# The first batch's attention in an order written out by hand, and its value tiles in three transfers

## The chip, the cores and the metric

One core of one Trainium2 chip runs the whole program. The metric is the device time of one execution in microseconds.

## The reference

Attention over four batches of eight heads, with 512 local and 32 global rows of 64 values per head, and then two MLPs. A local row attends to the 32 global keys and to the local keys at most 32 positions away; a global row attends to all 544 keys. All in float32:

```python
s_ll = np.where(np.abs(pos[:, None] - pos[None, :]) <= 32, scale * q_l @ k_l.T, -1e9)
out_l = softmax([scale * q_l @ k_g.T, s_ll]) @ [v_g, v_l]
out_g = softmax(scale * q_g @ [k_g, k_l].T) @ [v_g, v_l]
x = attention output, heads side by side          # 2176 tokens x 512
xn = x / sqrt(mean(x * x) + 1e-6) * rms_g
y = (silu(xn @ w_gate) * (xn @ w_val)) @ w_out     # 512 -> 1536 -> 512
out = leaky(y @ w_in) @ w_out2                     # 512 -> 2048 -> 512
```

## The kernel before, in words

The attention works on units: a unit is one pair of heads of one batch, so a batch has four units (`NP`) and eight half units, each of two tiles of 128 query rows (`half_unit`, L235). A half unit k runs these steps. `scores` (L243) multiplies keys and queries into two PSUM banks `sc` (L158, through `together`); then, for each of four tiles, DVE adds the mask and takes the minimum of the negated scores (L258, into `s_ring` and `mx`), and ACT takes the exponential with its row sum (L261). `norm` (L265) adds up the doubled columns and scales by the reciprocal sums (DVE, L268 to L276). `turned` (L279) transposes on PE into `pp` (L288, L290) and copies to SBUF as `pt` (L295). `values` (L302) multiplies with the value tiles into `po` (L158) and copies to `x_loc` (ACT, L319). `s_ring` has three buffers, PSUM eight banks in this phase.

The global queries go by pairs of units (`global_pair`, L324): scores `sa`, `sb`, their maxima on DVE (L347 to L349), two exponentials on ACT, a copy of 32 columns (L356), transposes (L371, L372), value products `pz`, and a transpose back.

`load` (L209) brings a unit in: two halves of keys and queries (`kq`, 352 KB each, three buffers), a value tile `va` shifted by 32 rows (three transfers, four buffers), a second one `vb` (three transfers, three buffers), and four transfers of 8 KB of global values into one of three zeroed tiles `vz` (L233). All transfers are issued on SP's queue, in order; a transfer whose buffer is not yet free holds those behind it.

The first batch's steps are listed in `ORDER` (L451): S, N, T, V for a half unit's four steps, G for a global pair's, L for loads, D for squares. A "+" puts the steps behind it into a list (`later`) that the next `flush` empties, and `flush` is called within the steps, between matmuls and what follows them. The scheduler that places the instructions may still move them on each engine by its own reckoning, within the dependencies and the edges that `pinned` and `together` add. During this phase four weight chunks of the first MLP are also made (`convert`, L670, calling `narrow`, L102): each 512 KB of float64 words becomes 256 KB of float32 (one ACT and two DVE instructions), which is stored; then the chunk two or so steps ahead is fetched (L654). The first batch's normalisation is begun too: squares on ACT (L486), rows times gain on ACT (L492), sums on DVE (L503), the square root (L527) and its reciprocal.

Then `mlp1` (L892) begins with the gate product of its first step (`pg`, L934), which reads the rows times gain `xg` and the converted weights `wf`. The attention of batches 1 to 3 runs between the products of `mlp1`, by the slots of `PLAN` (L454); the second MLP follows. The scores of the first batch's second global pair come with the end of the first batch, its other steps inside `mlp1` (`LAST_PAIR`).

## Time and profile before

| | us |
|---|---|
| median of three runs | 954.7 |
| lowest, highest | 954.43, 955.53 |
| the profiled execution's own time | 955.33 |
| its span, first to last instruction | 953.6 |
| PE busy in the span | 914.3 (96%) |
| DVE, ACT, POOL busy | 617.4, 464.7, 5.1 |
| mean granted clock of TensorE | 0.983 of full speed |

A line of the profile names an engine (PE matmul, PEld weight load, DVE, ACT, POOL, SP), the line of the kernel, the operation, and what it writes and reads. "Idle before <-releaser" is the time for which the engine stood still just ahead of an instruction, and what ended that. Instructions of one engine overlap a little, so the step from one start to the next is often shorter than the duration. The granted clock is a share of 2.4 GHz; 0.5 is 1.2 GHz. In a table of windows the columns are the window, its length, the busy time (and count) of PE, PEld, DVE, ACT and POOL, the granted clock, the share of the DMA engines' time and the rate in GB/s.

### The profile page before, as it was taken

The page shows a single profiled execution, that of the slowest core. Times are in us where ns is not written, and L with a number is a line of the kernel's source. Part 1 is how long each engine was busy: PE and PEld are TensorE (multiplying, and loading weights), DVE is VectorE, ACT ScalarE, POOL GpSimd, SP SyncE. Part 2 cuts the span into 40 slices and gives each one's busy share as a digit, 9 for nine tenths or more (in the row PEclk, how much of TensorE's full clock was granted, in tenths as well). Part 3 has the DMA queues.
Part 4 walks back from the last instruction along what each step waited for, and adds up shares of the span by engine and source line. Part 5 has one row for each costly group of instructions (what it writes and reads, how often), then busy time and mean ns, then how long its engine had stood idle before and what let it go on. Part 6 is the DMA issues. An engine that isn't in the chain of part 4 may idle for free.

```text
span 953.6 us, 14727 instructions
## 1 busy us (share of the span) xinstructions
PE 914.3 (96%) x5172; PEld 742.9 (78%) x5172; DVE 617.4 (65%) x1380; ACT 464.7 (49%) x988; POOL 5.1 (1%) x26
## 2 busy tenths in 40 slices
PE   6588989999999999999999999999999999999998
PEld 4445767777777777777799999888888888888886
DVE  5469887679767687765678776676656434445332
ACT  5566666456445556553643443445544324334331
POOL 2000000000000000000000000000000000000000
PEclk9798989999999999999999999999999999999999
DMA  5788796679787999897377766777522176641113
GB/s 174 232 283 287 249 310 233 211 248 351 268 312 262 380 320 410 315 408 270 116 241 257 250 184 225 239 258 272 214 89 89 44 265 219 235 164 56 44 48 108
DMA packets 93354, 217.78 MB, mean 228 GB/s; under 512 B 15840, under 2 KB 31200, under 8 KB 91232
## 3 DMA queue, kind: packets, MB, share of 16 engines
q1 hardware_dynamic: 93280, 216.84, 65.9%
q8 instruction: 41, 0.67, 0.3%
q14 instruction: 33, 0.27, 0.1%
HBM read 150.21 MB, written 66.58 MB: 227 GB/s over the span
## 4 chain that ended last, share of the span: by engine, by line
PE 81%; DMA 2%; DVE 2%; ACT 1%; issue 1%; SPq 0%; DVEq 0%; ACTq 0%
PE o L85 18%; PE pg L85 9%; PE yp L85 8%; PE pv L85 8%; PE px L85 4%; PE py L85 4%; PE pz L85 4%; PE yt L85 4%; PE sc L158 2%; PE pw L85 2%; PE tz L85 2%; PE ty L85 2%; PE tx L85 2%; PE po L158 2%; PE po L85 1%; PE pr L85 1%
## 5 line engine op out<-in xcount | busy, mean ns | idle before, releaser
L85 PE MATMUL o<-wr,d 128*128 128x512 f32 x768 | 174.4, 389 | 0.0
L85 PEld LDWEIGHTS o<-wr,d 128*128 128x128 f32 x768 | 144.2, 188 | 29.9
L85 PE MATMUL pg<-xh,w 128*128 128x512 f32 x272 | 91.2, 416 | 1.3 <-ACT xh L89 1.3
L85 PE MATMUL pv<-xh,w 128*128 128x512 f32 x272 | 87.1, 400 | 0.0
L85 PE MATMUL yp<-hsh,w 128*128 128x512 f32 x288 | 84.0, 398 | 0.7 <-ACT hsh L89 0.7
L261 ACT ACTIVATE s_ring<-s_ring,mx 128x224 f32<-128x224 f32 x128 | 60.4, 473 | 44.7 <-DVE mx L258 44.5
L92 DVE TENSOR_TENSOR d<-h,d 128x512 fp32r<-128x512 f32 x64 | 42.1, 687 | 33.9 <-ACT d L89 33.9
L85 PEld LDWEIGHTS yp<-hsh,w 128*128 128x128 f32 x288 | 53.1, 188 | 13.8 <-issue 1.6
L85 PEld LDWEIGHTS pg<-xh,w 128*128 128x128 f32 x272 | 49.5, 193 | 17.9 <-issue 5.0
L85 PEld LDWEIGHTS pv<-xh,w 128*128 128x128 f32 x272 | 49.9, 189 | 11.7 <-issue 1.3
L158 PE MATMUL sc<-kq 64*128 64x224 f32 x256 | 43.0, 419 | 14.6 <-DMA kq<-kqv 12.9
L89 ACT CAST d<-h 128x512 fp32r<-128x512 f32 x64 | 38.2, 618 | 37.0 <-PE o L85 37.0
L85 PE MATMUL pg<-xl,w 128*128 128x512 f32 x136 | 54.6, 402 | 0.5 <-DVE xl L92 0.5
L89 ACT CAST w<-wf 128x512 fp32r<-128x512 f32 x68 | 41.6, 615 | 26.3 <-PE pv L85 16.1
L258 DVE CUSTOM_DVE_ANT_0 s_ring<-sc,masks 128x224 f32<-128x224 f32 x128 | 42.7, 385 | 17.3 <-PE sc L158 17.3
L85 PE MATMUL pv<-xl,w 128*128 128x512 f32 x136 | 53.4, 392 | 0.0
L85 PE MATMUL yp<-hsl,w 128*128 128x512 f32 x144 | 48.7, 398 | 1.1 <-DVE hsl L92 1.1
L85 PE MATMUL pz<-ysb,wr 128*128 128x512 f32 x192 | 49.2, 391 | 0.0
L92 DVE TENSOR_TENSOR w<-wf,w 128x512 fp32r<-128x512 f32 x68 | 46.3, 686 | 2.3 <-ACT w L89 2.2
L158 PEld LDWEIGHTS sc<-kq 64*128 64x128 f32 x256 | 28.0, 210 | 22.7 <-DMA kq<-kqv 13.5
L92 DVE TENSOR_TENSOR wr<-wr 128x1024 fp32r<-128x1024 f32 x16 | 19.6, 1225 | 39.7 <-ACT wr L89 39.6
L1240 ACT ACTIVATE h<-h 128x1536 f32<-128x1536 f32 x16 | 23.8, 1488 | 42.9 <-DVE h L883 42.9
(225 smaller groups left out, 1772.2 us busy)
## 6 DMA issues: line engine op xcount, KB each, us to landing
w<-w_dram SPq DMA_DIRECT2D x72, 512.0 KB, 5.6
w<-w SPq DMA_DIRECT2D x36, 512.0 KB, 5.2
w_dram<-w SPq DMA_DIRECT2D x36, 512.0 KB, 4.2
w64b<-w SPq DMA_DIRECT2D x32, 512.0 KB, 7.6
w_dram<-wr SPq DMA_DIRECT2D x8, 1792.0 KB, 7.9
wr<-w_dram SPq DMA_DIRECT2D x8, 1792.0 KB, 7.3
kq<-kqv SPq DMA_DIRECT2D x32, 352.0 KB, 5.2
w_f<-wf SPq DMA_DIRECT2D x36, 256.0 KB, 4.8
```

Source lines behind the costliest of these rows:

```text
L85: nc.tensor.matmul(dst, lhs[a], rhs[b], start=first and i == 0, stop=last and i == 2, skip_group_check=onto)
L89: nc.scalar.copy(hi, src)
L92: nc.vector.tensor_tensor(out=lo, in0=src, in1=hi.bitcast(F32), op=ALU.subtract)
L158: x = nc.tensor.matmul(dst, lhs, rhs, start=start, stop=stop, skip_group_check=bool(onto))
L258: nc.vector.tensor_tensor_reduce(out=sp, in0=sc[j][:, i * KW:(i + 1) * KW], in1=mask_of(t), scale=-scale, scalar=3.0e38, op0=ALU.add, op1= ...
L261: x = nc.scalar.activation(out=sp, in_=sp, func=AF.Exp, bias=mx[:, c:c + 1], scale=-1.0, accum_out=sm[:, c:c + 1])
L1240: nc.scalar.activation(out=out, in_=x, func=AF.Prelu, alpha=0.01)
```

## The change

The first batch runs under a manual schedule: on PE, DVE, ACT, SP and POOL the instructions keep the order of the text, from the first loads to the end of `first_batch`. The text is the new list `FIRST`, one line for each half unit k: its normalisation (n), the score products two half units ahead (p), the value products of the one before (v), its transposes (t), the copy of the large transposes on ACT (c), the copy of the values before (x), minima and exponentials two ahead (e), the copy of the small transpose, now always on DVE (d); then global steps, loads, squares (q), their sums (s), rows times gain (g), the halves of a weight conversion (a: one ACT and one DVE instruction, o: the last DVE instruction and the store), the table load (r), the root (R). Three of the four conversions move to the end of the list; the loads of unit 3's keys and queries come right after the scores of the first global pair, before the middle of the list.

The two value tiles of a unit become one tile with four buffers, filled by three transfers rather than six. Row 0 to 31 of its first half is no longer the rotated local row, so the global pairs multiply a zeroed stretch there (a POOL memset in place of a DVE copy) and take the last 32 local rows from `ve`, which grows from 32 to 64 rows and from two transfers to four. The small transfers leave SP: the global values `vz` of units 0 and 1 are issued by ACT at the very start, all others by POOL, and so are the `ve`. The transposed global weights are copied back into the tile that they came from. Unit 5's keys and queries are loaded after the list.

```diff
+        narrow_or(dst, *narrow_parts(pool, raw, name, bufs))
+
+    def narrow_parts(pool, raw, name, bufs=2):
         c = pool.tile([P, DM], F32, tag="nar_c", bufs=bufs, name="nc_" + name)
         r = pool.tile([P, DM], U32, tag="nar_r", bufs=bufs, name="nr_" + name)
         nc.scalar.activation(out=c, in_=raw[:, :, 1].bitcast(F32), func=AF.Prelu, scale=2.0 ** -112,
                              alpha=-2.0 ** 32)
         nc.vector.tensor_scalar(out=r, in0=raw[:, :, 0], scalar1=2.0 ** -29, scalar2=7.0,
                                 op0=ALU.mult, op1=ALU.min)
+        return c, r
...
-    anchors = {}
+    anchors, manual = {}, []
 
     @contextmanager
     def pinned(names):
 
         with ExitStack() as st:
             for x in names.split("+"):
-                if x:
+                if x and not manual:
...
-        shape, tag = (([P, HC], "kq0"), ([P, HC], "kq1"), ([P, NT, P], "va"), ([P, NT, P], "vb"))[part]
-        x = units[u, part] = at.tile(shape, F32, tag=tag, bufs=4 if part == 2 else 3, name=f"{tag}_{u}")
         if part < 2:
+            x = units[u, part] = at.tile([P, HC], F32, tag=f"kq{part}", bufs=3, name=f"kq{part}_{u}")
             nc.sync.dma_start(out=x, in_=kqv[b, p][:, part * HC:(part + 1) * HC])
             return
+        x = at.tile([P, 2, NT, P], F32, tag="v", bufs=4, name=f"v_{u}")
+        units[u, 2], units[u, 3] = x[:, 0], x[:, 1]
         v = kqv[b, p][:, 2 * HC:].rearrange("p (t d) -> p t d", d=P)
-        if part == 2:
-            nc.sync.dma_start(out=x[W:P], in_=v[0:P - W])
-            nc.sync.dma_start(out=x[0:W, 1:NT], in_=v[P - W:P, 0:NT - 1])
-            nc.sync.dma_start(out=x[0:W, 0], in_=v[P - W:P, NT - 1])
-            return
-        nc.sync.dma_start(out=x[0:W], in_=v_b[b, p][SG + W:KB])
-        nc.sync.dma_start(out=x[W:2 * W], in_=v[P - W:P])
-        nc.sync.dma_start(out=x[2 * W:P], in_=v[W:P - W])
+        nc.sync.dma_start(out=x[2 * W:P], in_=v[W:P - W].unsqueeze(1).to_broadcast([2 * W, 2, NT, P]))
+        nc.sync.dma_start(out=x[0:W], in_=v_b[b, p][SG:KB].rearrange("(y r) t d -> r y t d", y=2))
+        nc.sync.dma_start(out=x[W:2 * W], in_=v.rearrange("(y r) t d -> r y t d", r=W)[:, 0:P // W:P // W - 1])
+        if u >= NP:
+            spaced(u, nc.gpsimd)
+
+    def spaced(u, queue):
+        b, p = divmod(u, NP)
         units[u, "g"] = vz_ring[u % 3]
         for j in range(2):
             for i in range(2):
                 r, c = SG * (2 * j + i), slice(j * D, (j + 1) * D)
-                nc.sync.dma_start(out=vz_ring[u % 3][r:r + SG, i, c], in_=v_b[b, p][0:SG, 0, c])
+                queue.dma_start(out=vz_ring[u % 3][r:r + SG, i, c], in_=v_b[b, p][0:SG, 0, c])
...
-        def scores():
+        def products():
             kq = units[u, k % 2]
-            sc = [bank(f"sc{j}" + tg, 2 * NP <= k < 2 * NP + 2) for j in range(2)]
+            sc = hold["sc"] = [bank(f"sc{j}" + tg, 2 * NP <= k < 2 * NP + 2) for j in range(2)]
...
+        def scores():
+            products()
+            flush()
+            exps()
...
+            transposes(j)
+            flush()
+            copies(j)
...
+        def copies(j):
+            w = (4 if j == 0 else 1) * P
+            pp = hold["pp", j][:, 0:w]
+            pt = hold[j] = at.tile([P, w], F32, tag=f"pt{j}", bufs=2, name=f"pt{j}" + tg)
+            on_act = j == 0 or b == 1
+            x = (nc.scalar.copy if on_act else nc.vector.tensor_copy)(pt, pp)
+
+        def values():
+            gathered()
             flush()
-            pp = pp[:, 0:w]
-            pt = hold[j] = at.tile([P, w], F32, tag=f"pt{j}", bufs=2, name=f"pt{j}" + tg)
-            on_act = j == 0 or b == 1 or b == 0 and k % 2
-            x = (nc.scalar.copy if on_act else nc.vector.tensor_copy)(pt, pp)
-            if k == 2 * NP - 1 and j == 1:
-
-                with tc.issue_after(x.ins):
-                    nc.scalar.activation(out=early_root, in_=eps, func=AF.Sqrt)
-
-        def values():
-            po = bank("po" + tg)
+            kept()
...
+        parts = {"P": products, "E": exps, "N": norm, "T": lambda: [transposes(j) for j in range(2)],
+                 "C": lambda: copies(0), "D": lambda: copies(1), "V": gathered, "X": kept}
+        return scores, norm, turned, values, parts
...
-            hold["ve"] = [at.tile([SG, P], F32, tag=f"ve{n}", bufs=1, name=f"ve{n}" + tg) for n in range(2)]
+            hold["ve"] = [at.tile([G2, P], F32, tag=f"ve{n}", bufs=1, name=f"ve{n}" + tg) for n in range(2)]
             for n in range(2):
-                nc.sync.dma_start(out=hold["ve"][n], in_=v_b[b, p0 + n][0:SG, 0])
+                nc.gpsimd.dma_start(out=hold["ve"][n][0:SG],
+                                    in_=kqv[b, p0 + n][P - W:P, 2 * HC + (NT - 1) * P:])
+                nc.gpsimd.dma_start(out=hold["ve"][n][SG:G2], in_=v_b[b, p0 + n][0:SG, 0])
...
-            g = hold["g"] = at.tile([P, NK], F32, tag="sg", name="sg" + tg)
+            g = hold["g"] = at.tile([P, (NT + 1) * P], F32, tag="sg", name="sg" + tg)
...
-            nc.vector.tensor_copy(g[:, 0:SG], g[:, S:S + SG])
+            nc.gpsimd.memset(g[:, 0:SG], 0.0)
...
-            nc.tensor.transpose(ph[0:SG, 0:P], g[:, S + SG:NK], ident)
+            nc.tensor.transpose(ph[0:G2, 0:P], g[:, S:NK], ident)
             flush()
-            gt = hold["gt"] = at.tile([P, (NT + 1) * P], F32, tag="gt", bufs=1, name="gt" + tg)
+            gt = g
             nc.scalar.copy(gt[:, 0:S], pg[:, 0:S])
-            nc.scalar.copy(gt[0:SG, S:], ph[0:SG, 0:P])
+            nc.scalar.copy(gt[0:G2, S:], ph[0:G2, 0:P])
...
-            return [item(t) for t in ORDER.split()]
+            return lambda t: half[int(t[1])][4][t[0].upper()]() if t[0].islower() else one(t)()
...
-    ORDER = ("S0 S1+N0+Q0 T0+N1 S2 V0 T1+N2 S3 V1+D0+L33 G01+G0n+L30+L31 T2+N3 S4 V2 T3+N4 S5 V3+D1 G02 "
-             "T4+N5 S6 G03 V4 T5+N6 S7 V5+D2+L40+L41 G04 T6+N7 V6+L42+L43 T7+L50+L51 V7+D3+L52+L53")
+    def first_batch():
+
+        do = attention(0)
+        squares, root, _, _, gained = norms[0]
+        parts = {}
+
+        def weights(t):
+            g, k = int(t[1]), int(t[2])
+            if t[0] == "a":
+                parts[g, k] = narrow_parts(mb, wraw[g, k], f"{k}_{g}")
+                return
+            wf[g, k] = mp.tile([P, DM], F32, tag="wf", bufs=7, name=f"wf{k}_{g}")
+            narrow_or(wf[g, k], *parts[g, k])
+            kept_weights(g, k)
+
+        adds = {}
+
+        def squared(t):
+            c = int(t[1])
+            squares(c)
+            adds[c] = deferred.pop()
+
+        def spread_later(t):
+            root()
+            adds["root"] = deferred.pop()
+
+        more = {"q": squared, "s": lambda t: adds[int(t[1])](), "g": lambda t: gained(int(t[1])), "a": weights,
+                "o": weights, "r": lambda t: nc.scalar.activation(out=early_root, in_=eps, func=AF.Sqrt),
+                "R": spread_later, "z": lambda t: spaced(NP - 1, nc.gpsimd)}
+        for t in FIRST.split():
+            (more.get(t[0]) or do)(t)
+            flush()
+        return adds["root"]
+
+    FIRST = ("p0 e0 p1 e1 "
+             "n0 p2 t0 c0 e2 d0 Q0 "
+             "n1 p3 v0 t1 c1 x0 e3 d1 G01 L30 L31 "
+             "n2 p4 v1 t2 c2 x1 z0 e4 d2 q0 s0 g0 L40 L41 "
+             "n3 p5 v2 t3 c3 x2 e5 d3 G0n G02 "
+             "n4 p6 v3 t4 c4 x3 e6 d4 a00 "
+             "n5 p7 v4 t5 c5 x4 e7 d5 o00 G03 r0 L42 "
+             "n6 v5 t6 c6 x5 q1 g1 d6 G04 "
+             "n7 s1 v6 t7 c7 x6 q2 d7 L52 "
+             "v7 s2 x7 q3 s3 g2 R0 g3 a01 o01 a10 a11 o10 o11")
...
-            1: "2:T0+N1;5:V0+L22+L23+L20 S2", 2: "2:T1+N2;5:V1+L21 S3",
-            3: "2:T2+N3;5:V2+L32+L33+L30 S4", 4: "0:G01+G0n;2:T3+N4;5:V3+L31 S5",
-            5: "0:G02;2:T4+N5;4:G03;5:V4+L42+L43+L40 S6", 6: "0:G04;2:T5+N6;5:V5+L41 S7",
-            7: "2:T6+N7;5:V6+L52+L53", 8: "0:G11+G1n;2:T7;5:V7+L50+L51", 9: "0:G12;1:G13;3:G14"}
+            1: "2:T0+N1;5:V0+L22+L20 S2", 2: "2:T1+N2;5:V1+L21 S3",
+            3: "2:T2+N3;5:V2+L32+L30 S4", 4: "0:G01+G0n;2:T3+N4;5:V3+L31 S5",
+            5: "0:G02;2:T4+N5;4:G03;5:V4+L42+L40 S6", 6: "0:G04;2:T5+N6;5:V5+L41 S7",
+            7: "2:T6+N7;5:V6+L52", 8: "0:G11+G1n;2:T7;5:V7+L50+L51", 9: "0:G12;1:G13;3:G14"}
...
+        def gained(c):
+            if c == 0:
+                xg.append(mp.tile([P, KC, NX], F32, tag="xh", bufs=2, name="xg"))
+            x = nc.scalar.activation(out=xg[0][:, c, 0:n], in_=x_loc[0][:, c, 0:n], func=AF.Copy,
+                                     scale=gcol[:, c:c + 1])
+            anchors["xg"] = x.ins
...
-    for x in vz_ring:
-        nc.gpsimd.memset(x, 0.0)
-    load(0, 0)
-    load(0, 1)
-    load(0, 2)
-    load(0, 3)
-    with nc.allow_non_contiguous_dma(reason="512 gains, one column a chunk"):
-        nc.sync.dma_start(out=gcol, in_=rms_g.rearrange("(c p) -> p c", p=P))
-    constants()
-    global_queries(0)
-    for u in (1, 2):
-        for part in range(4):
+    engines = {mybir.EngineType.PE, mybir.EngineType.DVE, mybir.EngineType.Activation, mybir.EngineType.SP}
+    norms[0] = normalise(0, 0, BLOCKS1[0])
+    manual.append(True)
+    with tc.manual_schedule(engines=engines | {mybir.EngineType.Pool}):
+        for u in range(2):
+            nc.gpsimd.memset(vz_ring[u], 0.0)
+            spaced(u, nc.scalar)
+        for u, part in ((0, 0), (0, 1), (1, 0), (0, 2), (1, 1), (1, 2)):
             load(u, part)
-    load(3, 2)
-    for g in range(2):
-        for k in range(3):
-            if g < W64[k]:
-                fetch(g, k)
-    norms[0] = normalise(0, 0, BLOCKS1[0])
-    for n, item in enumerate(attention(0, norms[0][0])):
-        item()
-        if n < 2:
-            flush()
-        if n == 20:
-            convert(0, 0)
-        if n == 25:
-            convert(0, 1)
+        constants()
+        global_queries(0)
+        nc.gpsimd.memset(vz_ring[2], 0.0)
+        spaced(2, nc.gpsimd)
+        with nc.allow_non_contiguous_dma(reason="512 gains, one column a chunk"):
+            nc.sync.dma_start(out=gcol, in_=rms_g.rearrange("(c p) -> p c", p=P))
+        for part in range(3):
+            load(2, part)
+        load(3, 2)
+        for g in range(2):
+            for k in range(3):
+                if g < W64[k]:
+                    fetch(g, k)
+        spread = first_batch()
+    manual.clear()
     flush()
     early = attention(1)
-    convert(1, 0)
-    norms[0][1]()
-    spread = deferred.pop()
     last_pair[NP // 2 - 1][0]()
     later(last_pair[NP // 2 - 1][1])
-    convert(1, 1)
+    load(NP + 1, 0)
+    load(NP + 1, 1)
```

## Rows read from the trace of the kernel before

**Rows 1.** Windows by stage: PE, PEld, DVE, ACT, POOL busy us (count); clock, DMA.

```profile
4.00:28.80 24.80, 18.66 (x186) 13.77 (x186) 16.28 (x82) 17.69 (x66) 1.83 (x10) 0.93 0.67 205
28.80:37.50 8.70, 0.03 (x2) 0.03 (x2) 2.61 (x8) 1.92 (x5) 0.00 (x0) 0.62 0.74 243
37.50:56.80 19.30, 15.03 (x177) 10.85 (x177) 10.33 (x37) 13.13 (x37) 0.00 (x0) 0.82 0.69 194
56.80:140.00 83.20, 75.11 (x378) 51.07 (x374) 71.72 (x176) 55.62 (x131) 0.00 (x0) 0.92 0.86 285
140.00:953.00 813.00, 805.42 (x4436) 667.19 (x4436) 516.25 (x1077) 375.05 (x753) 0.00 (x0) 1.00 0.64 224
```

**Rows 2.** Timeline of PE: start us, us, what, count, idle before it and its releaser.

```profile
15.47 1.03 PE L158 MATMUL sc<-kq 64*128 64x224 f32 x8
...
22.11 0.34 PE L158 MATMUL po<-pt,va 128*64 128x64 f32 x4 [1.11 <-ACT pt L295]
...
23.24 0.66 PE L288 MATMUL pp<-ident,s_ring 128*128 128x128 f32 x4
...
23.93 1.03 PE L158 MATMUL sc<-kq 64*128 64x224 f32 x8
...
37.47 1.87 PE L158 MATMUL sc<-kq 64*128 64x224 f32 x8 [8.71 <-DMA kq<-kqv]
...
56.77 3.70 PE L934 MATMUL pg<-xg,wf 128*128 128x512 f32 x8
```

**Rows 3.** Timeline of SP's DMA issues: start us, us, line, what is loaded, count.

```profile
4.66 2.11 SPq L233 DMA_DIRECT2D vz<-v_b  x4
...
34.31 1.84 SPq L218 DMA_DIRECT2D kq<-kqv  x4
```

**Rows 4.** Waits of SP's queue, 0 to 110 us: total us, times, longest us.

```profile
SPq L233 <- DMA w<-w: 2.7, 2, 1.5
```

**Rows 5.** Timeline of DVE: start us, us, line, operation.

```profile
28.80 0.29 DVE L295 COPY pt<-pp 128x128 f32<-128x128 f32 x1 [0.86 <-PE pp L290]
29.01 0.16 DVE L268 TENSOR_SCALAR sm<-sm 128x4 f32<-128x4 f32 x1
...
30.43 0.42 DVE L115 TENSOR_SCALAR nr<-w 128x512 uint32<-128x512 uint32 x1
...
39.37 0.39 DVE L258 CUSTOM_DVE_ANT_0 s_ring<-sc,masks 128x224 f32<-128x224 f32 x1 [7.92 <-PE sc L158]
...
40.31 0.39 DVE L258 CUSTOM_DVE_ANT_0 s_ring<-sc,masks 128x224 f32<-128x224 f32 x1
```

**Rows 6.** Timeline of ACT: start us, us, line, operation.

```profile
6.48 0.48 ACT L261 ACTIVATE s_ring<-s_ring,mx 128x224 f32<-128x224 f32 x1 [4.46 <-DVE mx L258]
...
39.80 0.48 ACT L261 ACTIVATE s_ring<-s_ring,mx 128x224 f32<-128x224 f32 x1 [9.08 <-DVE mx L258]
...
41.68 0.35 ACT L391 ACTIVATE xg_g<-pz_g,gm_g 128x128 f32<-128x128 f32 x1
...
51.24 1.28 ACT L299 ACT_TABLE_LOAD   x1
...
55.73 0.63 ACT L486 ACTIVATE sq<-xl 128x512 f32<-128x512 f32 x1
```

**Rows 7.** Waits of DVE, 0 to 56.8 us: total us, times, longest us.

```profile
DVE gm_g L347 <- PE sa_g L158: 1.6, 1, 1.6
```

**Rows 8.** Windows of 2 us in which loads were queued: columns as in Rows 1.

```profile
12.00:14.00 2.00, 2.00 (x16) 1.39 (x18) 1.63 (x7) 0.31 (x1) 0.00 (x0) 0.55 1.02 295
18.00:20.00 2.00, 2.00 (x27) 1.38 (x23) 1.08 (x9) 1.92 (x9) 0.00 (x0) 1.00 1.05 344
26.00:28.00 2.00, 1.90 (x30) 1.46 (x30) 1.94 (x10) 1.97 (x9) 0.00 (x0) 1.00 1.00 408
```

**Rows 9.** Windows after PE's first pause and in the first MLP: columns as in Rows 1.

```profile
10.40:14.00 3.60, 3.41 (x21) 2.41 (x23) 2.57 (x12) 1.53 (x6) 0.00 (x0) 0.53 0.97 312
...
70.00:100.00 30.00, 27.01 (x130) 18.41 (x129) 29.54 (x80) 22.30 (x58) 0.00 (x0) 0.89 0.82 284
```

More of the change, by code (lines that the diff above doesn't have):

```diff
@@ L155, in together @@
             with ExitStack() as st:
-                if last is not None:
+                if last is not None and not manual:
                     st.enter_context(tc.issue_after(last))
@@ L249, in scores, with exps @@
                           kq[halves[j], i * KW:(i + 1) * KW], True, True) for i in range(2) for j in (1, 0))
-            flush()
+        def exps():
+            sc = hold["sc"]
             s = hold["s"] = s_ring[k % 3]
@@ L281, in turned, with transposes @@
                 flush()
+            transposes(j)
+            flush()
+            copies(j)
+        def transposes(j):
             s = hold["s"]
-            pp = bank(f"pp{j}" + tg)
+            pp = hold["pp", j] = bank(f"pp{j}" + tg)
             v = s.rearrange("p (c k) -> p c k", k=SC)
-            w = (4 if j == 0 else 1) * P
             if j == 0:
@@ L290, in turned, with gathered @@
                 nc.tensor.transpose(pp[:, 0:P], hold["sg"].rearrange("p c k -> p (c k)"), ident)
-            flush()
-            pp = pp[:, 0:w]
-            pt = hold[j] = at.tile([P, w], F32, tag=f"pt{j}", bufs=2, name=f"pt{j}" + tg)
-            on_act = j == 0 or b == 1 or b == 0 and k % 2
-            x = (nc.scalar.copy if on_act else nc.vector.tensor_copy)(pt, pp)
-            if k == 2 * NP - 1 and j == 1:
-                with tc.issue_after(x.ins):
-                    nc.scalar.activation(out=early_root, in_=eps, func=AF.Sqrt)
-        def values():
-            po = bank("po" + tg)
+        def copies(j):
[6 more added lines that the diff above has]
+            gathered()
+            flush()
+            kept()
+        def gathered():
+            po = hold["po"] = bank("po" + tg)
             halves = [slice(j * D, (j + 1) * D) for j in range(2)]
@@ L314, in values, with kept @@
             together(products)
-            flush()
+        def kept():
+            po = hold["po"]
             if b not in x_loc:
@@ L320, in values @@
             anchors[f"x{k}"] = x.ins
-        return scores, norm, turned, values
+        parts = {"P": products, "E": exps, "N": norm, "T": lambda: [transposes(j) for j in range(2)],
+                 "C": lambda: copies(0), "D": lambda: copies(1), "V": gathered, "X": kept}
+        return scores, norm, turned, values, parts
     def global_pair(w):
@@ L371, in turned @@
                 nc.tensor.transpose(pg[:, c * P:(c + 1) * P], g[:, c * P:(c + 1) * P], ident)
-            nc.tensor.transpose(ph[0:SG, 0:P], g[:, S + SG:NK], ident)
+            nc.tensor.transpose(ph[0:G2, 0:P], g[:, S:NK], ident)
             flush()
-            gt = hold["gt"] = at.tile([P, (NT + 1) * P], F32, tag="gt", bufs=1, name="gt" + tg)
+            gt = g
             nc.scalar.copy(gt[:, 0:S], pg[:, 0:S])
-            nc.scalar.copy(gt[0:SG, S:], ph[0:SG, 0:P])
+            nc.scalar.copy(gt[0:G2, S:], ph[0:G2, 0:P])
         def values():
-            gt = hold["gt"]
+            gt = hold["g"]
             pz = bank("pz" + tg)
@@ L383, in values @@
                 for n, r in enumerate(halves):
-                    rows = slice(0, P if c < NT else SG)
+                    rows = slice(0, P if c < NT else G2)
                     v = units[us[n], 2][:, c, :] if c < NT else hold["ve"][n]
@@ L488, in squares @@
                 hold["sum"] = mb.tile([P, NX], F32, tag="ssum", name=f"ssum{i}")
-            if i == 0:
-                if c == 0:
-                    xg.append(mp.tile([P, KC, NX], F32, tag="xh", bufs=2, name="xg"))
-                x = nc.scalar.activation(out=xg[0][:, c, 0:n], in_=x_loc[0][:, c, 0:n], func=AF.Copy,
-                                         scale=gcol[:, c:c + 1])
-                anchors["xg"] = x.ins
             def add():
@@ L549, in scaled @@
             later(lambda: low(xs[i][1][:, c, 0:n], xn[:, 0:n], xs[i][0][:, c, 0:n]))
-        return squares, root, scaled, hold
+        return squares, root, scaled, hold, gained
     NI = len(BLOCKS1)
@@ L677, in convert, with kept_weights @@
             narrow(mb, wf[g, k], wraw[g, k], f"{k}_{f}")
-        nc.sync.dma_start(out=w1_f32[f][k], in_=wf[g, k])
+        kept_weights(g, k)
+    def kept_weights(g, k):
+        nc.sync.dma_start(out=w1_f32[step_of(g)[1]][k], in_=wf[g, k])
         if step_of(g + W64[k])[0] == 0:
```

2 lines of the change are left out of this document (1 added, 1 removed).

## The prediction

> **What bounds the kernel now.** I read the windows by stage first, then PE's waits in the stage that is weakest, then the queue that feeds it. From 140 us on PE is busy 805.4 of 813 us [rows 1]: nothing in this change can gain much there. From 56.8 to 140 us, the first MLP's opening, PE is busy 75.1 of 83.2. Before 56.8 us it is busy 18.7 of 24.8, then 0.03 of 8.7, then 15.0 of 19.3 [rows 1], and nothing in its first 4 us. So about 23 of the first 56.8 us are PE's idle time, and all of that lies in the first batch's attention, which the change rewrites. The first MLP's first product `pg` starts at 56.77 us [rows 2]; I forecast by how much that start moves.
>
> Two things make the idle time. The large one is a single wait of 8.71 us for unit 3's keys and queries, which end it at 37.47 us [rows 2]. SP issued that load only at 34.31 us [rows 3]: it stood behind small loads, and SP was itself held by weight transfers that had not landed [rows 4]. The other is the pace. Between the score products at 15.47 and 23.93 us lie two half units, so one takes 4.23 us [rows 2], though PE's own work for one is 1.03 us of scores, 1.13 of value products (22.11 to 23.24) and 0.69 of transposes (23.24 to 23.93), 2.85 in all; PE stood 1.11 us ahead of the value products, for ACT's copy of the transposes just made [rows 2].
>
> **The change part by part.**
>
> *The order.* Each line of the new list gives the engines work of three half units, so that no engine waits for what was begun in the same line, the small copy `d` excepted. A line costs DVE 1.42 us of normalisation (29.01 to 30.43), four minima at 0.31 a step (39.37 to 40.31 is three steps), 1.25, and 0.21 for the small copy (28.80 to 29.01) [rows 5]: 2.88. PE needs 2.85, ACT 1.88 for the exponentials (39.80 to 41.68) [rows 6], which leaves it a microsecond for its two copies. So a line takes 2.9 us where it took 4.23, and DVE and PE share the limit. I walk along it:
> - Start. The first exponential came at 6.48 us [rows 6]. Now ACT first issues eight small transfers; at the 0.53 us that SP takes for one (four in 2.11) [rows 3] that is 4.2 us, with POOL's memset ahead of them and a table load of 1.28 [rows 6] about 6.5 us. No row shows a transfer issued by ACT: at best it costs nothing (the keys land no sooner), at worst I allow 1.5 us, the longest hold of SP's queue [rows 4]. I take 0, because SP's rows are the nearest.
> - Two half units of exponentials end at 6.5 + 2 x 1.88 = 10.3; the first normalisation starts after one, at 8.4. Lines 0 and 1 take DVE to 14.2.
> - The first global pair's scores hang on line 1. DVE waited 1.6 us for these products in the second pair [rows 7], and the maxima take 0.7: line 2 starts at 16.5, line 3 at 19.4, line 4, after 0.3 of global reciprocals, at 22.6.
> - Line 4 needs unit 3's keys. SP now issues them behind 7.3 MB (seven `kq` halves with this one, four value tiles, five weight chunks, small ones), all queued early. At the rates of windows in which such loads were queued, 295 GB/s for values, 344 for keys, 408 for weights [rows 8], 2.1 MB, 2.5 MB and 2.6 MB take 7.1, 7.3 and 6.4 us, the small ones about one; from 2 us on, and with one us to be reported, they land at 24.7. The wait of 8.7 us shrinks to 2.1.
> - Line 5 starts at 22.6 + 2.9 + 2.1 + 0.3 (half a conversion) = 27.9, line 6 at 31.4 (0.6 for the conversion's other half), line 7, without minima ahead, at 33.8.
> - The end has no neighbour to hide in: normalisation 1.4, a wait of 1.9 because ACT's table load (1.28) delays line 6's copies, transposes 0.7, copy 0.5, value products 1.1, copy 0.3, then two pairs of squares and gains at 1.04 each (55.73 to the `pg` that follows at 56.77 [rows 6, 2]): 41.8.
> - The second pair's scores, 2 us of PE, stood ahead of `pg` before; now they come when the root's products are out, at 40.3, so `pg` starts at 42.3.
> - Clock. In 10.4 to 14.0 us the granted clock was 0.53, the 1.2 GHz level, after a pause of PE; PE was busy 3.4 us there [rows 9], and at 2.4 GHz the same work takes about half. The pauses around 8 us and for unit 3's keys remain: I add 2 us. `pg` starts at 44.3.
>
> *Values in three transfers.* Bytes stay at 512 KB a unit. Three issues and four small ones leave SP for each unit, some 3.5 us at 0.5 each, and this is what lets the sum above take the loads as limited by bytes. Gain beyond that: none.
>
> *Small loads by POOL.* POOL issues four `vz` and four `ve` transfers and then the memset that the first pair's transposes wait for, at 21 us; its constants end at 7 us. At SP's 0.53 the eight take 4.2 us, done at 11.3. No row shows a transfer issued by POOL. They cost nothing as long as one takes under (21 - 7) / 8 = 1.75 us; `vz` of unit 3 is needed ten us later.
>
> *The rest.* The memset replaces a DVE copy of 0.2 us; `gt` in the place of `g` makes the next pair wait for value products that are long done; the wider `ve` product is the same instruction over 64 rows. All at nothing, within 0.5 us. Two conversions that came before `pg` now follow it: four DVE instructions, 1.9 us. `pg` itself (3.70 us [rows 2]) covers the one that the next product needs. DVE is full later (29.5 of 30 us between 70 and 100 us [rows 9]), so if they slip as far as that they cost 1.9. I take 0, for `pg` stands directly ahead.
>
> *Sum.* `pg` moves from 56.77 to 44.3 us, 12.5 us. The work behind it is the same, bound by PE and DVE, so I let it all move. The profiled execution took 955.33 us, so 942.8; it lies 0.6 above the median of 954.7, so 942.2 for the median, rounded to 942.5.
>
> **The rivals.**
>
> *A, loads set the pace.* If the early queue moves only 243 GB/s, the mean of the 8.7 us around the long wait [rows 1], 7.3 MB from 2 us on land at 32 us, 7.3 later than in the sum: 949.5. At 205 GB/s, the mean of 4 to 28.8 us [rows 1], they land at 37.6, as late as before, and nothing is gained. For it: these are the means there. Against it: in those stretches SP was issuing small loads or waiting, and windows with loads queued show 295 to 408 [rows 8]. Chance 0.15, of which 0.04 at no gain.
>
> *B, the gain is given back.* Weights reach the first MLP by the same DMA engines, busy 0.86 of that stage [rows 1], and DVE is full in 30 us of it [rows 9]. Should the shifted stage wait for weights or for the conversions, half is lost: 948.5. Against it: 285 GB/s [rows 1] is below what queued weights reach [rows 8]. Chance 0.10.
>
> *C, the order does not shorten the half unit.* If handovers between the engines keep a line at 4.2 us, only the long wait shrinks, by 6.6 us, less one us or so for the start: 949.5. For it: a fixed order stalls behind its slowest piece, and ACT issues transfers first. Against it: before, the wait was for a copy of the same half unit [rows 2], and that distance is doubled. Chance 0.07.
>
> *D, slower.* POOL's transfers run late in a row, with the memset behind them. If one takes c us, the first pair's transposes, and behind them all of PE's order, wait until 7 + 8c; the loss is 8c - 14, and over c = 3.3 it exceeds the 12.5 gained. At c = 4 the time is 960. Against it: the smallest issue in the rows is 0.53 [rows 3], and POOL has nothing else to do; for it, nothing in this trace, since POOL issues no transfer here. Chance 0.08.
> The Trainium skill, "SBUF — State Buffer", section "SBUF: two separate sides" (its trap "DVE blocks DMA"), says that a transfer from POOL's queue needs descriptors that POOL writes through a port which some DVE instructions lock, and gives 620 ns alone against about 3100 ns beside such an instruction. By that figure, taken for every one of the eight, the loss would be about 11 us and the time about 953; no run here shows it.
>
> **How the numbers follow.** A measurement of this kernel can tell about 0.2%, 1.9 us, from no change. The forecast has 0.60; its own range is 938 (no clock loss, no wait for unit 3) to 946 (ACT's start and the conversions at their upper bounds). With A, B and C the range is 937 to 951. Faster: 0.60 + 0.11 + 0.10 + 0.07 = 0.88. Within 0.2%: 0.04. Slower: 0.08.
>
> **What would show it.** Right: score products about 2.9 us apart, `pg` starting at 42 to 46 us, a wait for `kq` under 3 us, 56.8 to 140 us moved as a whole. Wrong: A by a wait for `kq` beyond 5 us; B by a stage from `pg` on that is longer than 83 us for the same work; C by score products 4 us apart without such a wait; D by PE or ACT waiting for POOL.

## The result, and the profile after

The changed kernel took 945.06 us (median of four runs, 942.53 to 946.54) beside 954.57 us for the kernel before on the same chip (954.1 to 955.53): a ratio of 0.9896, interval 0.9873 to 0.992. The profiled execution took 944.61 us, its span is 942.8, 10.8 shorter than before.

The windows by stage of the changed kernel, columns as in [rows 1]:

```profile
4.00:28.80 24.80, 17.97 (x157) 13.78 (x157) 17.25 (x82) 16.75 (x59) 8.22 (x24) 0.86 1.01 288
28.80:37.50 8.70, 7.34 (x70) 5.59 (x71) 3.65 (x17) 4.03 (x15) 2.21 (x4) 0.61 0.29 107
37.50:56.80 19.30, 14.83 (x156) 9.40 (x157) 13.82 (x41) 16.90 (x42) 5.95 (x13) 1.00 0.75 207
56.80:140.00 83.20, 77.94 (x445) 55.03 (x443) 76.99 (x196) 59.03 (x145) 7.77 (x17) 0.98 0.93 314
```

The hole of 28.8 to 37.5 us is nearly full, as forecast (PE busy 7.34 of 8.7 us, though at a clock of 0.61). But the stage from 56.8 us, which I had only meant to move, changed too: PE is busy 77.94 us of 83.2 (75.11 before), the clock is 0.98 (0.92), the DMA engines move 314 GB/s (285) [rows 1].

PE's timeline around the first batch's end, and the first product of the MLP's second block:

```profile
30.16 1.87 PE L156 MATMUL sc<-kq 64*128 64x224 f32 x8 [3.36 <-DMA kq<-kqv]
...
49.02 2.84 PE L1000 MATMUL pg<-xg,wf 128*128 128x512 f32 x6
...
53.41 1.16 PE L598 MATMUL rb<-rs,ident 128*128 128x128 f32 x8 [1.54 <-ACT sg_g L371]
...
55.27 3.60 PE L1000 MATMUL pv<-xg,wf 128*128 128x512 f32 x8
...
200.86 0.73 PE L85 MATMUL pg<-xh,w 128*128 128x512 f32 x2 [1.04 <-ACT xh L89]
```

`pv` and the second block's product in the kernel before:

```profile
61.20 3.60 PE L934 MATMUL pv<-xg,wf 128*128 128x512 f32 x8
...
210.13 0.73 PE L85 MATMUL pg<-xh,w 128*128 128x512 f32 x2 [1.04 <-ACT xh L89]
```

So `pg` moved by 7.75 us (from 56.77 [rows 2]), not by 12.5. It now runs in two parts, with the spread of the root (`rb`) and a wait of 1.54 us between, so that `pv` behind it moved by 5.93 only; the second block moved by 9.27. Of the 10.8 us, 5.9 come from the first batch, 3.3 from the stage behind it, 1.5 from what follows 200 us.

Where the first batch lost against the forecast: ACT's and SP's timelines at the start.

```profile
1.08 6.83 ACTq L232 DMA_DIRECT2D vz<-v_b  x8
...
2.47 0.44 ACTq L232 DMA_DIRECT2D vz<-v_b  x1
...
4.22 0.32 ACTq L232 DMA_DIRECT2D vz<-v_b  x1
...
7.94 1.28 ACT L262 ACT_TABLE_LOAD   x1 [7.94 <-DMA vz<-v_b]
9.23 0.48 ACT L262 ACTIVATE s_ring<-s_ring,mx 128x224 f32<-128x224 f32 x1
```

```profile
2.12 0.74 SPq L220 DMA_DIRECT2D v<-kqv  x1
3.94 0.34 SPq L221 DMA_DIRECT2D v<-v_b  x1
4.86 0.32 SPq L222 DMA_DIRECT2D v<-kqv  x1
6.70 0.35 SPq L215 DMA_DIRECT2D kq<-kqv  x1
7.90 0.62 SPq L220 DMA_DIRECT2D v<-kqv  x1
...
21.13 5.09 SPq L215 DMA_DIRECT2D kq<-kqv  x4
```

The first row holds all eight of ACT's transfers; the two below it are the fourth and the fifth of these. One issue took ACT 0.32 to 0.44 us, but it stood between the last ones, so the eight took 6.83 us. The table load could only follow: the first exponential came at 9.23 us instead of 6.48 [rows 6]. While ACT issued, SP's own issues stood up to 1.8 us apart. DVE's timeline shows the walk: the start of the normalisation in lines 0 and 2 to 7.

```profile
11.23 0.17 DVE L274 TENSOR_SCALAR sm<-sm 128x4 f32<-128x4 f32 x1 [2.53 <-ACT s_ring L262]
...
21.05 0.16 DVE L274 TENSOR_SCALAR sm<-sm 128x4 f32<-128x4 f32 x1
...
24.03 0.16 DVE L274 TENSOR_SCALAR sm<-sm 128x4 f32<-128x4 f32 x1
...
27.32 0.15 DVE L274 TENSOR_SCALAR sm<-sm 128x4 f32<-128x4 f32 x1
...
35.77 0.17 DVE L274 TENSOR_SCALAR sm<-sm 128x4 f32<-128x4 f32 x1
...
39.35 0.16 DVE L274 TENSOR_SCALAR sm<-sm 128x4 f32<-128x4 f32 x1
...
41.82 0.16 DVE L274 TENSOR_SCALAR sm<-sm 128x4 f32<-128x4 f32 x1
```

POOL had issued everything early, at 0.50 to 0.53 us each (the memset is what the first pair's transposes wait for):

```profile
10.19 0.50 POOL L357 DMA_DIRECT2D ve_g<-v_b  x1
10.67 0.14 POOL L375 MEMSET sg_g<- 128x32 f32 x1
```

### The profile page after: what moved, and what is told of

It is laid out like the page before. It is cut to its first block, busy times and chain, and to the rows that moved or that the text cites. A ratio compares the mean times of both kernels' runs of the same rounds, so it can differ in the third digit from the quotient of the medians.

```text
span 942.8 us, 14764 instructions
## 1 busy us (share of the span) xinstructions
PE 911.3 (97%) x5172; PEld 742.1 (79%) x5172; DVE 618.0 (66%) x1376; ACT 463.1 (49%) x984; POOL 50.4 (5%) x122
## 4 chain that ended last, share of the span: by engine, by line
PE 78%; DMA 4%; DVE 1%; ACT 1%; issue 1%; SPq 1%; ACTq 0%; DVEq 0%
PE o L85 18%; PE yp L85 8%; PE pg L85 8%; PE pv L85 7%; PE px L85 4%; PE py L85 4%; PE pz L85 4%; PE yt L85 4%; DMA w64b<-w 2%; PE pw L85 2%; PE tz L85 2%; PE ty L85 2%; PE tx L85 2%; PE sc L156 2%; PE po L156 2%; PE po L85 1%
## 5 line engine op out<-in xcount | busy, mean ns | idle before, releaser
L85 PE MATMUL yt<-hst,w 128*128 128x320 f32 x288 | 42.9, 310 | 1.0 <-DMA w<-w_dram 0.7
```

Of the source, the lines that this page charges most:

```text
L85: nc.tensor.matmul(dst, lhs[a], rhs[b], start=first and i == 0, stop=last and i == 2, skip_group_check=onto)
```

## The experiments

All ratios are to the kernel before, run on the same chip with the kernel named. "Changed" is the changed kernel, 0.9896.

### 1. The small values at the start by POOL

```diff
-            spaced(u, nc.scalar)
...
-        spaced(2, nc.gpsimd)
+        for u in range(3):
+            spaced(u, nc.gpsimd)
```

> The eight small transfers of units 0 and 1 are issued by POOL behind its constants, not by ACT. Theory (ACT's issues set the late start: they took 6.83 us, and SP was held with few loads in flight beside them): the first exponential comes at about 6.5 us instead of 9.23, SP's first loads are issued without holds, and everything behind moves by 2.5 to 4 us: 941 to 942.5 us. Rival (the start is bound by when keys and masks land, ACT only happened to be busy): the first exponential stays near 9 us and the time at 945. Second rival (POOL now issues 16 transfers in a row, and the first value products wait for the global values): the value products of unit 0 wait for POOL's transfers, gain under 1 us.

944.08 us, ratio 0.9886 [0.9859, 0.9914], which the intervals do not part from the changed kernel. The start is mended, and the gain is swallowed at the next wait. ACT's and PE's timelines:

```profile
6.33 0.48 ACT L262 ACTIVATE s_ring<-s_ring,mx 128x224 f32<-128x224 f32 x1 [4.31 <-DVE mx L259]
```

```profile
30.01 1.87 PE L156 MATMUL sc<-kq 64*128 64x224 f32 x8 [6.92 <-DMA kq<-kqv]
```

PE now waits 6.92 us for unit 3's keys instead of 3.36 and goes on at nearly the same time as before, 30.01 us (30.16). The start was late, but the keys set the pace: `pg` starts at 48.23 us, 0.8 earlier. The second rival's sign showed too: PE waited 1.45 us for the global values that POOL now issues.

### 2. The first five weight chunks behind unit 3's keys

```diff
-        for g in range(2):
-            for k in range(3):
-                if g < W64[k]:
-                    fetch(g, k)
...
-             "n1 p3 v0 t1 c1 x0 e3 d1 G01 L30 L31 "
+             "n1 p3 v0 t1 c1 x0 e3 d1 G01 L30 L31 f00 f01 f02 f10 f11 "
```

> The first five weight chunks are fetched behind unit 3's keys and queries instead of ahead of them. Theory (unit 3's keys land late because 2.6 MB of weights are queued ahead): PE's wait of 3.36 us for them falls under 1 us, and the 1.2 GHz stretch that follows it goes too (1.5 us more): 940 to 942 us. Rival (they are late because SP may issue them only once the first global pair's scores are done, so the order of the queue behind that changes nothing): the wait stays above 2.5 us, 944 to 946. Second rival: the weights, now late themselves, hold the conversions and the first MLP; slower than 946.

939.5 us, ratio 0.9836 [0.9803, 0.987], a little under the theory's 940 to 942. In PE's timeline the products of unit 3 follow at once:

```profile
26.56 1.03 PE L156 MATMUL sc<-kq 64*128 64x224 f32 x8
...
47.22 3.18 PE L1000 MATMUL pg<-xg,wf 128*128 128x512 f32 x6
```

They take 1.03 us, not 1.87: without the pause PE also keeps the 2.4 GHz level. The five chunks, 2.6 MB, were what stood between the keys and their place in the queue. But `pg` starts only 1.8 us earlier than in the changed kernel (47.22, 49.02): behind a later wait of 1.66 us, for ACT's copy of the transposes, PE ran the end of the batch at the 1.2 GHz level (granted clock 0.50 from 42 to 47 us).

### 3. All small loads back on SP

```diff
-            spaced(u, nc.gpsimd)
+            spaced(u, nc.sync)
...
-                nc.gpsimd.dma_start(out=hold["ve"][n][SG:G2], in_=v_b[b, p0 + n][0:SG, 0])
+                nc.sync.dma_start(out=hold["ve"][n][SG:G2], in_=v_b[b, p0 + n][0:SG, 0])
```

> All small transfers (global values and the global pairs' rows) go back to SP's queue; the order by hand and the three value transfers stay. Theory (SP's queue is short of issue time early, and small loads hold the large ones there; and the stage after 57 us gained because SP no longer carries them): the keys of units 2 and 3 land later, PE waits 3 to 6 us more, but ACT starts 2.7 us earlier; together 945 to 949 us, with the stage from the gate product to 140 us some 3 us longer than now. Rival (where the small transfers are issued does not matter beyond ACT's late start): 942 to 943.

954.55 us, ratio 0.9992 [0.9976, 1.0008]: the whole gain is gone, more than the theory's 945 to 949, with the written order and the three transfers still in place. `pg` still starts 3.7 us earlier than in the kernel before (53.06, 56.77), and nothing of that reaches the end. PE's waits of 0 to 140 us:

```profile
PE sc L156 <- DMA kq<-kqv: 14.4, 3, 7.6
```

### 4. Minimum steps one half unit ahead instead of two

```diff
-    FIRST = ("p0 e0 p1 e1 "
-             "n0 p2 t0 c0 e2 d0 Q0 "
-             "n1 p3 v0 t1 c1 x0 e3 d1 G01 L30 L31 "
...
+    FIRST = ("p0 e0 "
+             "n0 p1 t0 c0 e1 d0 Q0 "
+             "n1 p2 v0 t1 c1 x0 e2 d1 "
...
```

> Score products, minima and exponentials run one half unit ahead instead of two, all else as in the changed kernel. Theory (the distance of two is what takes the handovers between the engines out of the line): a line takes 4 us or more where it now takes 3.0 to 3.5, eight lines cost 5 to 8 us more: 949 to 953. Rival (the distance does not matter, only the fixed order and the loads do): within 1.5 us of 945.

950.36 us, ratio 0.9949 [0.9929, 0.9969]. PE's timeline shows lines 4.97 and 4.98 us apart, with PE waiting for DVE's normalisation:

```profile
18.80 0.63 PE L298 MATMUL pp<-ident,s_ring 128*128 128x128 f32 x4 [0.52 <-DVE s_ring L280]
...
23.77 0.63 PE L298 MATMUL pp<-ident,s_ring 128*128 128x128 f32 x4 [2.23 <-DVE s_ring L280]
...
34.26 0.63 PE L298 MATMUL pp<-ident,s_ring 128*128 128x128 f32 x4 [1.72 <-DVE s_ring L280]
...
39.24 0.63 PE L298 MATMUL pp<-ident,s_ring 128*128 128x128 f32 x4 [2.23 <-DVE s_ring L280]
```

In a written order the distance of two is worth 0.5%, with a reservation: this list also moves the first global pair's scores and unit 3's loads one line later, and what these cost was not separated. `pg` starts at 57.58 us, later than in the kernel before (56.77), and the time is shorter all the same.

### 5. Experiments 1 and 2 together

The edit is the two diffs above.

> Both at once: the first eight small transfers by POOL, and the first five weight chunks behind unit 3's keys. Theory (the early start was worth under a microsecond alone only because the wait for unit 3's keys swallowed it; without that wait it comes through): first exponential at 6.4 us, no wait for keys over 2 us, the gate product starts 2 to 3 us earlier than with the keys first alone (47.2 us), at 44 to 45.5; ratio to the kernel before 0.979 to 0.983. Rival (the tail, bound by ACT, sets the end, so the start is still hidden): the gate product stays at 47, ratio 0.983 to 0.986.

938.39 us, ratio 0.9816 [0.9773, 0.9859]; `pg` at 42.36 us, no wait for unit 3's keys. Taken alone, the start had moved `pg` by 0.8 us; with the keys in place nothing swallows it, and line 7 begins 1.7 us earlier than in experiment 2 (DVE's first instruction of it at 34.77 us, 36.49 there). `pg` is 4.9 us earlier, but most of what lies behind line 7 is the clock: the second pair's scores, in experiment 2 and here, ran at the 1.2 and at the 2.4 GHz level.

```profile
44.75 1.95 PE L156 MATMUL sa_g<-kq,bd 128*64 128x256 f32 x8
```

```profile
41.01 1.06 PE L156 MATMUL sa_g<-kq,bd 128*64 128x256 f32 x8
```

In device time the interval does not part this kernel from experiment 2.

### 6. The new loads alone, in the scheduler's order of before

The kernel before with three value transfers and the small loads issued by POOL; the order of the first batch is left as it was.

```diff
+        nc.sync.dma_start(out=x[2 * W:P], in_=v[W:P - W].unsqueeze(1).to_broadcast([2 * W, 2, NT, P]))
...
-                nc.sync.dma_start(out=vz_ring[u % 3][r:r + SG, i, c], in_=v_b[b, p][0:SG, 0, c])
+                queue.dma_start(out=vz_ring[u % 3][r:r + SG, i, c], in_=v_b[b, p][0:SG, 0, c])
...
+            spaced(u, nc.gpsimd)
```

> The loads of the change alone (three value transfers, small loads by POOL, the global pairs' changes), with the order of the kernel before left to the scheduler. Theory A (half or more of the gain is SP's queue set free): unit 3's keys are issued before 28 us, PE's longest wait falls from 8.7 to 3 to 5 us, and the first MLP runs as in the changed kernel: ratio 0.989 to 0.995. Theory B (the order by hand is what gains; loads only let it): ratio 0.997 to 1.0. Theory C (the order gives nothing once the loads are free): ratio 0.988 to 0.991, as the changed kernel.

947.17 us, ratio 0.9896 [0.986, 0.9931]: the same ratio as the changed kernel, without its order. And this with a bad start of its own: POOL put its transfers among the masks, the last of which was done at 13.3 us, and PE's timeline shows 7.52 us of waiting for it:

```profile
14.63 1.08 PE L292 MATMUL pp<-ident,s_ring 128*128 128x128 f32 x4 [7.52 <-DVE s_ring L278]
```

SP issued unit 3's keys at 22.74 us (34.31 before [rows 3]), and PE never waited for them.

### 7. Only the later small loads back on SP

```diff
-            spaced(u, nc.gpsimd)
+            spaced(u, nc.sync)
...
-                nc.gpsimd.dma_start(out=hold["ve"][n][SG:G2], in_=v_b[b, p0 + n][0:SG, 0])
+                (nc.sync if w else nc.gpsimd).dma_start(out=hold["ve"][n][SG:G2], in_=v_b[b, p0 + n][0:SG, 0])
```

> The first batch as in the changed kernel, but the small loads of all later units and global pairs on SP's queue again. Theory (the stage behind the gate product gained some 4 us because small loads that wait for a buffer no longer stand in SP's queue ahead of weights): the gate product starts at 49 us as now, and the stage up to 140 us takes 3 to 5 us longer: ratio 0.993 to 0.996. Rival (that stage gained by where the conversions stand, or by the clock): ratio 0.988 to 0.991, as the changed kernel.

953.96 us, ratio 0.9962 [0.9941, 0.9982]. About 6 us are lost (0.9962 against 0.9896). In the profiled runs 1.5 us of the loss lie ahead of `pg` (50.52 us, 49.02 in the changed kernel) and 4.1 between `pg` and the second block (206.46, 200.86). The longest wait of a small load in SP's queue, 0 to 140 us:

```profile
SPq L355 <- PE pz_g L156: 10.5, 1, 10.5
```

A load of 16 KB waits 10.5 us on SP until PE has read the buffer that it overwrites, and everything that SP was to issue stands behind it. Yet this wait is not the price. In the changed kernel SP stands as long in the same stretch, ahead of the first conversion's store, for DVE. That kernel's wait (26 to 40 us) and its issues, then the issues here:

```profile
SPq L744 <- DVE sm L274: 12.2, 1, 12.2
```

```profile
39.45 0.33 SPq L744 DMA_DIRECT2D w_f<-wf  x1
...
90.43 1.42 SPq L717 DMA_DIRECT2D w<-w  x2
```

```profile
39.79 0.34 SPq L355 DMA_DIRECT2D ve_g<-kqv  x1
...
40.85 0.35 SPq L744 DMA_DIRECT2D w_f<-wf  x1
...
96.59 1.26 SPq L717 DMA_DIRECT2D w<-w  x2
```

The store goes out 1.4 us later, the fifteenth weight fetch behind it 6.2 us later. So the delay grows in the stage that I had let move unchanged, while SP issues small loads among the weights. How it divides between their issue, their waits and engines that are themselves late was not separated.

### 8. Two conversions behind the second pair's scores

Experiment 5 with the conversions of chunks (1,0) and (1,1) taken out of the first batch's list and put behind the next pair.

```diff
-             "v7 s2 x7 q3 s3 g2 R0 g3 a01 o01 a10 a11 o10 o11")
+             "v7 s2 x7 q3 s3 g2 R0 g3 a01 o01")
...
+    convert(1, 0)
+    convert(1, 1)
```

> As both at once, and the last two conversions come behind the second pair's scores and exponentials, outside the fixed order. Theory (in the changed kernel PE stood 1.5 us in the middle of the gate product, for exponentials that stood behind these conversions on ACT): that wait goes, and the value product starts 1 to 1.5 us earlier; ratio 0.001 to 0.0015 below both at once. Rival (DVE, full from 70 to 100 us, gets the two conversions later and gives it back): the same as both at once, or above.

939.57 us, ratio 0.9821 [0.9784, 0.9858]: no gain. The wait for the spread of the root (1.54 us ahead of `rb` above) stayed at 1.58. Where those conversions stand makes no difference that the interval shows.

### 9. Experiment 6 with its loads mended

The masks before POOL's transfers, the weight chunks behind unit 3's keys, and still the scheduler's order.

```diff
+    with tc.manual_schedule(engines={mybir.EngineType.Pool}):
+        constants()
+        for u in range(3):
+            spaced(u, nc.gpsimd)
...
+                        with tc.issue_after(anchors["kq"]):
+                            fetch(g, k)
```

> The scheduler's own order of before with the new loads, and with two mends: POOL builds the masks ahead of its value transfers (in the loads-alone kernel the masks were done at 13.3 us), and the first five weight chunks go out behind unit 3's keys. Theory (the order written by hand is itself worth time once the loads are good): the units still walk at 4 to 5 us a line instead of 3.0 to 3.5, pg is at 47 to 50 us, and the time is 943 to 946 (ratio 0.987 to 0.990). Rival (the loads are everything and any order would do): pg at 42 to 44 and 938 to 940 (ratio 0.981 to 0.983), as the changed kernel with both corrections (938.39).

943.22 us, ratio 0.9862 [0.9834, 0.9891]. The time is the theory's, the ratio just under its 0.987 to 0.990, though `pg` is even later than it said:

```profile
51.76 3.70 PE L943 MATMUL pg<-xg,wf 128*128 128x512 f32 x8
```

### 10 and 11. Each half of the loads alone, on the kernel before

Ten: the later small loads by POOL, the six value transfers kept.

```diff
-                nc.sync.dma_start(out=vz_ring[u % 3][r:r + SG, i, c], in_=v_b[b, p][0:SG, 0, c])
+                (nc.gpsimd if u >= NP else nc.sync).dma_start(out=vz_ring[u % 3][r:r + SG, i, c], in_=v_b[b, p][0:SG, 0, c])
...
-                nc.sync.dma_start(out=hold["ve"][n], in_=v_b[b, p0 + n][0:SG, 0])
+                (nc.gpsimd if w else nc.sync).dma_start(out=hold["ve"][n], in_=v_b[b, p0 + n][0:SG, 0])
```

> The kernel before with one part of the change alone: the spaced values of batches 2 on and the global pairs' values from the second pair on are issued by POOL instead of SP; the first batch and its six value transfers stay. Theory (these small loads hold SP's queue behind instructions that are not ready): 947 to 951, ratio 0.990 to 0.995, pg still at 56 to 57 us, and the stage 56.8 to 140 has a granted clock above 0.90 and a DMA rate above 290 GB/s. Rival (they hurt only together with the joined value transfers): 954 to 957, ratio 0.998 to 1.002.

956.47 us, ratio 1.0014 [0.9995, 1.0033]. My theory fell: nothing is gained.

Eleven: three value transfers and all small loads on SP, as against experiment 6:

```diff
-            spaced(u, nc.gpsimd)
+            spaced(u, nc.sync)
...
-                nc.gpsimd.dma_start(out=hold["ve"][n][SG:G2], in_=v_b[b, p0 + n][0:SG, 0])
+                nc.sync.dma_start(out=hold["ve"][n][SG:G2], in_=v_b[b, p0 + n][0:SG, 0])
```

> The kernel before with the values in three transfers instead of six and nothing else of the change that bears on queues: the spaced values and the global pairs' values stay on SP, the scheduler's order stays. Theory (fewer transfers alone give little, the place of the small ones gives the gain): 953 to 957, ratio 0.997 to 1.001. Rival (half the value transfers gone from SP lets every later load go sooner): 948 to 951, ratio 0.991 to 0.995.

957.19 us, ratio 1.0024 [0.9995, 1.0053]: nothing either. In both the first batch keeps its hole; PE's timeline of ten and of eleven:

```profile
38.06 1.87 PE L158 MATMUL sc<-kq 64*128 64x224 f32 x8 [8.72 <-DMA kq<-kqv]
```

```profile
35.59 1.87 PE L158 MATMUL sc<-kq 64*128 64x224 f32 x8 [7.16 <-DMA kq<-kqv]
```

Experiment 6, which has both and takes the first batch's small loads off SP too, has no such wait and gains 1%.

### 12. Both corrections once more

The kernel of experiment 5, unchanged.

> The changed kernel with both corrections (its first small values issued by POOL behind the constants, the first five weight chunks behind unit 3's keys) once more, in five rounds. Theory: 937 to 940, ratio 0.980 to 0.984, faster than before and than the changed kernel (945.06). Rival (its first figure of 938.39 was a lucky one): 943 or more.

937.15 us (933.34 to 940.73), ratio 0.9804 [0.9777, 0.983]: experiment 5 is confirmed, and this version beats both kernels, the one before by about 18 us and the changed one by about 9 (0.9804 against 0.9896). PE's timeline:

```profile
40.85 2.84 PE L1000 MATMUL pg<-xg,wf 128*128 128x512 f32 x6
...
190.25 0.73 PE L85 MATMUL pg<-xh,w 128*128 128x512 f32 x2 [1.03 <-ACT xh L89]
```

## Why the prediction was right, and where not

The forecast of 942.5 us lies 2.6 us below what was measured, 945.06, and the range holds it: 9.5 us came of some 12 forecast. The sign and the place were right, but two terms were wrong in opposite directions, and part of the agreement is luck: `pg` moved 4.7 us less than the 12.5 forecast, and the end 3.0 us more than `pg`. Of the four signs that I had set for being right, the first came only where neither the clock nor the keys stood in the way (score products at 19.95 and 23.21 us, 3.26 apart); `pg` at 49.02 us lies beyond 42 to 46, the wait of 3.36 us for keys beyond 3, and the stage up to 140 us did not move as a whole.

**What held.** "A line takes 2.9 us": the lines of 21.05 and 24.03 us are 2.98 apart, the next 3.29. Lines 5 to 7 were forecast 3.5 and 2.4 apart and came 3.58 and 2.47 apart. The way from line 7 to `pg` was 8.5 us before the clock's 2; it took 7.2. Experiment 4 supports that the distance of two makes this pace: with one, a line takes 5.0, and PE waits for the normalisation. Rival C is refuted. So is rival D: one issue by POOL is 0.50 to 0.53 us, its memset was done at 10.8 us, and nothing waited for it. The 3100 ns that the Trainium skill ("SBUF — State Buffer", section "SBUF: two separate sides") gives for a transfer beside certain DVE instructions was not seen in these issues: the four that POOL issued from 21.89 to 23.90 us took 0.50 each, with DVE busy in all of the 2.01 us. Whether one of those DVE instructions ran beside them, no run here shows.

**"Start ... I take 0" failed.** The first exponential came 2.75 us late, beyond my bound of 1.5. The row that I took was SP's 0.53 us an issue. An issue on ACT was no dearer, but ACT stood between the last of them: eight took 6.83 us instead of 4.2, with the table load behind them as in the sum. The bound rested on a misread row too: 1.5 us is SP's longest hold by weights [rows 4], but the same queue was held 3.3 us for PE (`SPq L233 <- PE po L158: 3.3, 1, 3.3`). Experiment 1 shows that this step alone was worth only 0.8 us of `pg` here: the keys swallowed the rest.

**"They land at 24.7" failed, and mending it alone gains more than mending the start.** Unit 3's keys ended PE's wait at 30.16 us. The rate was the miss: in 4 to 28.8 us the DMA engines, at a share of 1.01, moved 288 GB/s, not the mix of 295 to 408 that I took from short windows [rows 8]. The gaps between SP's issues at the start were not: in experiment 1 they are gone, the rate is 286 GB/s, and the wait ends at 30.01 us. Rival A had the mechanism, and its mark (a wait beyond 5 us) was hidden only because line 4 was itself 4.7 us late: with the start mended the wait is 6.92. Experiment 2 shows the order of the loads to be the cause of the wait: with 2.6 MB moved behind the keys, the wait is gone. The time falls by 5.6 us (945.06 to 939.5), of which `pg` shows only 1.8; where the rest comes from was not shown.

**"I add 2 us" for the clock was too little.** It fell where I had said, after both pauses: behind each, at 14.02 and 30.16 us, eight score products took 1.87 us, as at the 1.2 GHz level. Line 2 began 9.82 us after line 0 where I had 8.1, and PE's work from 30.16 to the next scores at 35.12 us took 4.96, where that from 19.95 to 23.21 took 3.26. By these rows the two falls cost some 3.4 us, an estimate.

**"The work behind it is the same, so I let it all move" failed in the good direction.** `pv` moved 5.9 us, the end 10.8. I costed the small loads by their issue, 0.5 us each, and wrote "gain beyond that: none". Experiment 7 prices the later ones alone at about 6 us of the changed kernel, most of it behind `pg`. By what path was not shown: the long wait of experiment 7 stands in place of one that SP has there anyway; experiment 6 gains its 1% with SP held 10.0 us by a value load; and on the kernel before the same loads are worth nothing (experiment 10). Rival B, a stage that gives the gain back, had the wrong sign.

**What the parts are worth.** The prediction gave nearly everything to the order. The experiments say otherwise: with small loads on SP the order gains nothing that the intervals show (experiment 3, 0.9992; experiment 11, such loads without it, 1.0024); the loads alone gain all that the change showed (experiment 6, 0.9896). Nor is the start of `pg` the measure that I took it for: in experiment 3 it is 3.7 us earlier than before and gains nothing, in experiment 4 later than before and the time still falls 0.5%. The order pays only when its loads are in time: with mended loads in both, the scheduler's order gives 0.9862 [0.9834, 0.9891] and the written one 0.9804 [0.9777, 0.983], about 5.5 us, with `pg` at 51.76 and 40.85.

**What stays open.** How the small loads slow the stage behind the first batch, and why neither half of the loads alone gains anything there. In the profiled run of experiment 11 the second block began 5.1 us earlier than before, at 205.05, and 3.5 of these were gone at the end; where they went was not settled, and that kernel's runs scatter by 13 us (953.31 to 966.82). Experiment 10's profiled run was its slowest, 963.29 us, and decides nothing beyond the wait shown. The granted clock of 56.8 to 140 us was 0.92 before, 0.98 in the changed kernel, 0.94 in experiment 7 and 1.00 in experiment 11; whether it makes the difference there or follows from it is not shown. Also not tried: the written order with six value transfers.

## What to carry to other kernels

Before you price a load by its wait in a queue that issues in order, ask what the queue would do without it: here it would have stood for a store. Take the loads off and measure, in the kernel that is to keep the change, for the same loads were worth 0.6% in one kernel and nothing in another. An order written out by hand is worth only as much as its latest load; before costing such an order, list what stands ahead of each load, byte by byte, and put what is needed first in front. And when two waits lie in a row, removing the first lengthens the second (from 3.36 to 6.92 us here) until that one's cause is gone too.

## What was not expected of the hardware

- One issue took 0.32 to 0.44 us on ACT's queue, though eight took 6.83 with the time between them, 0.50 to 0.53 on POOL's, and 0.32 to 0.74 on SP's in the same stretch.
- While ACT's eight transfers were out, SP's issues stood apart: `v` at 3.94 and 4.86, `kq` at 6.70. With the same transfers on POOL (experiment 5) SP issued these at 2.91, 3.53 and 4.00 us. ACT's issues of 4.22, 5.11 and 6.96 us each follow one of SP's by 0.25 to 0.28 us. A second queue is not needed for a gap: in experiment 3, where SP issues them all, it stands from 5.81 to 7.28 us. What the two queues share, no run here shows.
- One kernel ran at two clocks in the same place: experiments 5 and 12 are the same program, and from 10 to 14 us the granted clock was 0.62 in one and 1.00 in the other, after PE's waits of 1.86 and 1.49 us. Their `pg` starts are 1.5 us apart.
- A full share of the DMA engines is not a rate. Two windows of the changed kernel, columns as in [rows 1]:

```profile
10.00:20.00 10.00, 7.21 (x56) 5.26 (x56) 6.16 (x28) 6.69 (x27) 0.81 (x3) 0.66 1.04 250
20.00:28.00 8.00, 6.12 (x81) 4.65 (x79) 7.66 (x36) 7.20 (x27) 1.98 (x4) 1.00 1.03 364
```

The engines are full in both, and move 250 GB/s in the first, with value tiles among the loads that SP had just issued, and 364 in the second, with weights and keys.
